# Attention and gated MLP on one core: the fifth pair of heads split for the product with V

## The chip, the cores and the metric

The kernel runs on one core of one Trainium2 chip. The metric is device time in microseconds; the median of 3 runs before the change is 799.14 us (799.07 to 799.27). The engines are named as the profile names them: PE (TensorE, with PEld for its weight loads), DVE (VectorE), ACT (ScalarE), POOL (GpSimd) and SP (SyncE, which issues most transfers).

## The reference

```python
def _attn_ref(q, k, v, f):                       # q, k, v: 8 x 8 x 576 x 64
    scores = (1 / sqrt(D)) * q @ k.T
    cum = cumsum(log(clip(f, 1e-4, 1)))
    scores = where(causal, -1e9, scores + cum[..., :, None] - cum[..., None, :])
    attn = exp(scores - max(scores))
    attn = attn / (sum(attn) + 1e-9)
    return attn @ v

def _moe_ref(x, w_in, w_spatial, b_spatial, w_out):   # x: 8 x 576 x 512, d_ff 1024
    h = relu(x @ w_in)
    u, v = h[..., :512], h[..., 512:]
    v_n = (v - mean(v)) / sqrt(var(v) + 1e-6)
    v_s = einsum('ts,bsd->btd', w_spatial, v_n) + b_spatial[None, :, None]
    return (u * v_s) @ w_out
# result: _moe_ref of attn_out, its heads laid side by side
```

## The kernel before

The 64 heads are worked in 32 pairs `P`, four to a batch, and each batch's gated MLP (`moe`) follows on its four pairs. A pair goes through `scores` for each of its two heads (four tiles of 128 to 512 key columns, on PE into PSUM tiles `sc`, then DVE takes maximum and mask at L345 and ACT the exponential at L347, into `tt`), `scores_tail` for the last 64 queries of both heads (`tl`), `transposes` (PE turns `tt` into PSUM tiles `tp`), `evac` (the tiles `tp` go to SBUF), and `attend`, the product with V, into `x0` and `x1`. POOL divides the probabilities by their sums at L355, L375 and L378. In batch 0 there are three buffers for `sc` and for `tp`, later two.

The product with V is done in one of two ways. Pairs below `NF` keep probabilities (`ef`) and V (`vraw`) in float32; each tile `tp` is copied by either DVE or ACT, in turn (L386), and each matmul stands in the trace as two records. From `NF` on, both are split into a rounded and a remaining part: ACT casts `tp` to `eh` (L390), DVE subtracts it to get `el` (L391), ACT casts V (L321) and POOL subtracts (L322), which gives `vt` with hi and lo of each head side by side. Then `eh` and `el` are each multiplied with `vt`, and the two halves of the result, on different partitions of PSUM, are added by one more DVE instruction for each of `x0` and `x1` (L452), beyond the L450 that all pairs have.

While attention runs, PE's MoE matmuls (`ps`) lie between its steps. The weights `w_in` and `w_out` come as float64 and are converted piece by piece (`conv64`: L162 on ACT, L163 to L169 on DVE, L171 on POOL, L172 on ACT, L173 on POOL), so that DVE has this work besides its own until about 160 us. The last four pieces are those of `w_out`, which the tiles of the output product (`ps<-wo`) need.

The program is written with generators: `step` calls attention and `moe` in turn, by their progress. But the order of instructions on each engine is set by a scheduler, which goes by its own times of the instructions. Each engine then works its list in order. `after` ties the start of some instructions to marks such as the exponential of a given pair.

Of the kernel before, what the change touches and what calls it, by code (L numbers as in the profile page):

```python
# [16 lines left out]
DRAM = bass.MemoryType.DRAM  # L17

BIG = 1.0e9
NF = 5  # L20
NQ = 4
LEAD = 0.25
S = 576
# [15 lines left out]
def attn_gmlp_kernel(ctx: ExitStack, tc: tile.TileContext, qk, v, f, w_in, w_sp, b_sp, w_out, out):  # L39
# [268 lines left out]
    def read_vals(P):  # L308
        tag = "vt" if P < NF and P % 2 else "vraw"
        vts[P] = wk.tile([128, 5, 2, D], F32, name="vraw", tag=tag)  # L310
        after(SY.dma_start(out=vts[P], in_=v[P]), ("dma", P, 1))

    def prep_v(P):
        for p in range(P, min(P + 2, NF)) if P < NF else (P,):
            if p not in vts:
                read_vals(p)
        if P < NF:
            return
        vraw = vts[P]
        vt = wk.tile([128, 5, 4, D], F32R, name="vt", tag="vt")  # L320
        A.copy(vt[:, :, 0:4:3, :], vraw)  # L321
        G.tensor_tensor(out=vt[:, :, 1:3, :], in0=vraw, in1=f32(vt[:, :, 0:4:3, :]), op=ALU.subtract)  # L322
        vts[P] = vt
# [34 lines left out]
    def scores_tail(P):  # L358
# [14 lines left out]
        V.reciprocal(sm[:, 0:1], sm[:, 0:1])  # L373
        if P >= NF:
            G.tensor_scalar(out=tl[:, S:640], in0=tl[:, TL:S], scalar1=sm[:, 0:1], scalar2=1.0,  # L375
# [8 lines left out]
    def evac(P, ps, sel):  # L384
        if P < NF:
            (V.tensor_copy if nev[0] % 2 == 1 else A.copy)(sel(ET["f"]), ps)  # L386
            nev[0] += 1
            return
        h_ap, l_ap = sel(ET["h"]), sel(ET["l"])
        A.copy(h_ap, ps)  # L390
        V.tensor_tensor(out=l_ap, in0=ps, in1=f32(h_ap), op=ALU.subtract)  # L391

    def transposes(P, h):
        if P == NF and h == 0:
            ET["h"] = cst.tile([128, 2, 1600], F32R, name="eh", tag="eh")
            ET["l"] = cst.tile([128, 2, 1600], F32R, name="el", tag="el")
        for c in range(NB):
            n = 512 - 128 * c
            tp = PS['t'].tile([128, 512], F32, name="tp")
            for i in range(c, NB):  # L400
                T.transpose(out=tp[:, (i - c) * 128:(i - c + 1) * 128],  # L401
                            in_=tt[h][:, TOFF[i] + 128 * c:TOFF[i] + 128 * c + 128], identity=ident)
            e0 = EOFF[c]
            evac(P, tp[:, 0:n], lambda e: e[:, h, e0:e0 + n])
            yield 107 * (NB - c)
# [309 lines left out]
```

## Time and profile before

| | |
|---|---|
| median of 3 runs | 799.14 us (799.07 to 799.27) |
| profiled execution, its own time | 797.53 us |
| its span | 795.7 us, granted clock 0.993 |
| busy | PE 778.9, DVE 556.6, ACT 534.9, POOL 476.4 us |
| PE, records of the float32 product with V | 140, from 20.9 to 104.7 us |
| PE, records of the split product | 378 with `eh`, 324 with `el`, from 118.4 us on |

A line of the trace gives start, duration, engine, line, operation, result and operands, with `x` and the count where equal ones follow each other; a bracket names idle time ahead and what ended it. Durations of matmuls overlap, so work on PE is counted from one start to the next.

### The profile page before, as it was taken

To read this page: it belongs to the slowest core of one execution; us is meant where nothing else is said; L and a number is where in the kernel's file an instruction comes from. 1 tells how busy PE (TensorE), PEld (TensorE's weight loads), DVE (VectorE), ACT (ScalarE), POOL (GpSimd) and SP (SyncE) were. 2 spreads that over 40 slices of the span, in tenths; PEclk is the share of its full clock that TensorE was granted. 3 is DMA by queue.
4 is the path that set the end of the run, shared out by engine and by line. 5 is a ranking of instruction groups with operands and counts; after the bars stand their busy time and mean duration, and the time that the engine had idled before them with its cause. 6 is when DMAs were issued, how large, how long until landed. Compare 5 with 4: busy or idle time off the path is not lost.

```text
span 795.7 us, 15502 instructions
## 1 busy us (share of the span) xinstructions
PE 778.9 (98%) x4980; PEld 702.3 (88%) x4981; DVE 556.6 (70%) x1665; ACT 534.9 (67%) x1418; POOL 476.4 (60%) x660
## 2 busy tenths in 40 slices
PE   8999989899999999999999999999999999999997
PEld 4767779798999989998999989999899988998996
DVE  7889778975767667766866668766787658674421
ACT  7787678675777777667766668766686767764431
POOL 5777798664865647465655647554776537643251
PEclk9999999999999999999999999999999999999999
DMA  9967744566454565365454555564555465320001
GB/s 246 239 185 185 188 119 121 119 168 171 103 123 119 153 152 142 102 148 136 104 143 129 133 145 114 131 170 135 141 134 138 108 164 134 78 75 14 28 1 67
DMA packets 41713, 103.48 MB, mean 130 GB/s; under 512 B 6831, under 2 KB 8879, under 8 KB 41568
## 3 DMA queue, kind: packets, MB, share of 16 engines
q1 hardware_dynamic: 41306, 101.96, 49.7%
q8 instruction: 40, 0.66, 0.4%
q10 hardware_dynamic: 326, 0.53, 0.3%
q14 instruction: 41, 0.34, 0.1%
HBM read 39.42 MB, written 10.68 MB: 63 GB/s over the span
## 4 chain that ended last, share of the span: by engine, by line
PE 86%; DVE 6%; ACT 3%; POOL 2%; issue 2%; DMA 1%; ACTq 0%; POOLq 0%; DVEq 0%
PE ps L260 45%; PE sc L260 16%; PE x L260 12%; PE tp L401 8%; PE tp L260 2%; PE tp L414 2%; DVE tt L345 1%; POOL tt L355 1%; DVE el L391 1%; DVE xl L450 1%; DVE wa L163 0%; ACT eh L390 0%; DVE vx L545 0%; ACT tt L347 0%; ACT hi L278 0%
## 5 line engine op out<-in xcount | busy, mean ns | idle before, releaser
L355 POOL TENSOR_SCALAR tt<-tt,sm 128x128 f32<-128x128 f32 (+3 forms) x256 | 142.0, 573 | 74.9 <-DVE sm L351 56.4
L345 DVE CUSTOM_DVE_ANT_0 tt<-sc,zm 128x128 f32<-128x128 f32 (+3 forms) x256 | 122.8, 486 | 85.0 <-PE tp L401 63.4
L390 ACT CAST eh<-tp 128x512 fp32r<-128x512 f32 (+1 forms) x270 | 111.4, 426 | 75.4 <-PE tp L401 50.2
L347 ACT ACTIVATE tt<-tt,nm 128x128 f32<-128x128 f32 (+3 forms) x256 | 144.4, 565 | 23.7 <-DVE nm L345 21.9
L391 DVE TENSOR_TENSOR el<-tp,eh 128x512 fp32r<-128x512 f32 (+1 forms) x270 | 127.2, 485 | 26.2 <-ACT eh L390 23.8
L401 PE MATMUL tp<-ident,tt 128*128 128x128 f32 x640 | 111.6, 277 | 4.1 <-DVE el L391 4.1
L260 PE MATMUL sc<-ta 128*128 128x128 f32 (+1 forms) x336 | 109.1, 330 | 2.5 <-DVE nm L345 2.0
L260 PE MATMUL sc<-tb 68*128 68x128 f32 (+1 forms) x336 | 106.2, 320 | 0.0
L260 PE MATMUL x<-eh,vt 128*128 128x320 f32 (+4 forms) x378 | 102.5, 287 | 0.0
L593 POOL TENSOR_TENSOR gl<-u,gh 128x256 fp32r<-128x256 f32 x64 | 47.7, 745 | 87.7 <-ACT gh L592 78.1
L260 PE MATMUL ps<-xh,win 128*128 128x256 f32 (+1 forms) x464 | 99.3, 304 | 0.4 <-ACT u L570 0.3
L280 POOL TENSOR_TENSOR lo<-raw,hi 128x640 fp32r<-128x640 f32 (+1 forms) x56 | 84.2, 1525 | 16.1 <-ACT hi L278 15.9
L260 PE MATMUL ps<-win,xh 128*128 128x512 f32 x296 | 90.6, 396 | 0.0
L260 PE MATMUL x<-el,vt 128*128 128x256 f32 x324 | 90.1, 303 | 0.0
L401 PEld LDWEIGHTS tp<-ident,tt 128*128 128x128 f32 x640 | 76.3, 141 | 14.2 <-issue 2.7
L449 ACT CAST xh<-x 64x256 fp32r<-64x256 f32 (+1 forms) x128 | 49.8, 394 | 42.3 <-PE x L260 40.3
L260 PEld LDWEIGHTS ps<-xh,win 128*128 128x128 f32 x464 | 76.3, 192 | 2.0 <-ACT u L570 0.9
L260 PE MATMUL ps<-sph,vnh 128*128 128x256 f32 (+1 forms) x240 | 73.2, 305 | 0.4 <-ACT o L618 0.4
L260 PEld LDWEIGHTS x<-eh,vt 128*128 128x128 f32 x378 | 71.3, 190 | 2.5 <-POOL vt L322 0.3
L260 PE MATMUL ps<-wo,gh 128*128 128x512 f32 x224 | 71.9, 405 | 0.0
L260 PEld LDWEIGHTS sc<-ta 128*128 128x128 f32 x336 | 64.3, 191 | 8.6 <-DVE nm L345 4.5
L260 PE MATMUL ps<-sph,vnl 128*128 128x256 f32 (+1 forms) x240 | 71.6, 298 | 0.0
(178 smaller groups left out, 1916.4 us busy)
## 6 DMA issues: line engine op xcount, KB each, us to landing
raw<-in_dram SPq DMA_DIRECT2D x28, 608.0 KB
ta<-hi SPq DMA_DIRECT2D x56, 304.0 KB
vraw<-in_dram SPq DMA_DIRECT2D x32, 320.0 KB
tb<-hi SPq DMA_DIRECT2D x56, 160.0 KB
ta<-lo SPq DMA_DIRECT2D x56, 160.0 KB
out_dram<-o SPq DMA_DIRECT2D x32, 256.0 KB
ta<-hi SPq DMA_DIRECT2D x56, 144.0 KB
tb<-lo SPq DMA_DIRECT2D x56, 144.0 KB
```

The lines of the kernel that those rows point to most:

```text
L260: last['mm'] = T.matmul(o, l, r, start=st, stop=sp)
L280: G.tensor_tensor(out=lo[:, c], in0=raw[:, c], in1=f32(hi[:, c]), op=ALU.subtract)
L345: V.tensor_tensor_reduce(out=t, in0=sc[:, 0:n], in1=zm[:, 640 - n:640], scale=-0.125, scalar=3.0e38, op0=ALU.add, op1=ALU.min, accum_out=n ...
L347: last["exp"] = last["exp", P, h, i] = A.activation(t, t, AF.Exp, bias=nm[:, i:i + 1], scale=-1.0, accum_out=se[:, i, 0:1])
L355: G.tensor_scalar(out=t, in0=t, scalar1=sm[:, i:i + 1], scalar2=1.0, op0=ALU.mult, op1=ALU.mult)
L390: A.copy(h_ap, ps)
L391: V.tensor_tensor(out=l_ap, in0=ps, in1=f32(h_ap), op=ALU.subtract)
L401: T.transpose(out=tp[:, (i - c) * 128:(i - c + 1) * 128], in_=tt[h][:, TOFF[i] + 128 * c:TOFF[i] + 128 * c + 128], identity=ident)
L414: T.transpose(out=tp[:, j * 128:(j + 1) * 128], in_=tl[:, c * 128:(c + 1) * 128], identity=ident)
L449: last[P, h] = A.copy(hi, ps[m0:m0 + 64, 0:n])
L450: V.tensor_tensor(out=lo, in0=ps[m0:m0 + 64, 0:n], in1=f32(hi), op=ALU.subtract)
L593: G.tensor_tensor(out=gl[j][:, 0:256], in0=g[:, 0:256], in1=f32(gh[j][:, 0:256]), op=ALU.subtract)
```

## The change

```diff
-NF = 5
+NF = 4
```

`NF` is the number of pairs whose product with V is done in float32. With 4, pair 4 (the fifth, the first of batch 1) is split as all later pairs are. For its two heads 14 float32 matmuls (28 records) become 26 split ones. Its ten evacuations on DVE or ACT (five each) become ten on ACT and ten on DVE, with one small DVE cast (L423). Added besides are a POOL instruction on `tl` (L375), the V cast on ACT and the subtraction on POOL, and four L452 on DVE. The tiles `eh` and `el` are first used one pair earlier. The tile `vt` takes the buffer in which pair 3 has its V. No transfer is added or removed.

The scheduler's order changes from the end of pair 3 (the first transposes of pair 4) on; PE's last 2139 rows are the same in both.

On POOL, at the first head of pair 4, before; `wa` and `win` belong to the conversion of `w_in`, `raw`, `hi` and `lo` to the split of queries and keys of a later pair:

```order
L173 TENSOR_TENSOR win_842<-wa,win_842 128x512
L171 TENSOR_TENSOR wa<-w_942,wa 128x512
L173 TENSOR_TENSOR win_949<-wa,win_949 128x512
L280 TENSOR_TENSOR lo<-raw,hi 128x640
L280 TENSOR_TENSOR lo<-raw,hi 128x576
L543 TENSOR_TENSOR mv<-mv,lnc 128x1
```

The same place now:

```order
L173 TENSOR_TENSOR win_840<-wa,win_840 128x512
L171 TENSOR_TENSOR wa<-w_941,wa 128x512
L322 TENSOR_TENSOR vt<-vraw,vt 128x5x128
L280 TENSOR_TENSOR lo<-raw,hi 128x640
L280 TENSOR_TENSOR lo<-raw,hi 128x576
L173 TENSOR_TENSOR win_948<-wa,win_948 128x512
```

The subtraction that makes `vt` of pair 4 stands behind L171, and the second L173 moves behind the split of queries and keys.

On PE, at the same time, before, from the end of a block of MoE matmuls on:

```order
L260 MATMUL ps<-win_578,xl 128x512
L401 MATMUL tp<-ident,tt_67 128x128 x2
L260 MATMUL x_1129<-ef,vraw 128x256
L401 MATMUL tp<-ident,tt_67 128x128
L260 MATMUL x_1129<-ef,vraw 128x128
L260 MATMUL sc<-ta 128x384
L260 MATMUL sc<-tb 128x384
L260 MATMUL sc<-ta 128x512
L260 MATMUL sc<-tb 128x512
L414 MATMUL tp<-ident,tl 128x128 x3
```

The same place now:

```order
L260 MATMUL ps<-win_578,xl 128x512
L260 MATMUL sc<-ta 128x384
L260 MATMUL sc<-tb 128x384
L260 MATMUL sc<-ta 128x512
L260 MATMUL sc<-tb 128x512
L401 MATMUL tp<-ident,tt_67 128x128 x3
L260 MATMUL x_1142<-eh,vt 128x256
L260 MATMUL x_1142<-el,vt 128x256
L260 MATMUL x_1142<-eh,vt 128x128
L260 MATMUL x_1142<-el,vt 128x128
L260 MATMUL sc<-ta 128x288
```

The product with V moves behind the two widest scores products, and the tail's scores and transposes stand behind it.

On PE again, later, between the first two tiles of the output product (`wo_1564` and `wo_1595` are the third pieces of `w_out`, before and now), before:

```order
L401 MATMUL tp<-ident,tt_67 128x128 x3
L260 MATMUL sc<-tb 128x256
L260 MATMUL ps<-wo_1564,gh 128x512
L260 MATMUL ps<-wo_1564,gl 128x512
L260 MATMUL ps<-wo_1564,gh 128x512
L260 MATMUL ps<-wo_1564,gl 128x512
L260 MATMUL sc<-ta 128x384
L260 MATMUL sc<-tb 128x384
L401 MATMUL tp<-ident,tt_67 128x128 x2
L260 MATMUL sc<-ta 128x512
```

The same steps of a head now:

```order
L401 MATMUL tp<-ident,tt_67 128x128 x3
L260 MATMUL sc<-ta 128x384
L260 MATMUL sc<-tb 128x384
L260 MATMUL sc<-ta 128x512
L260 MATMUL sc<-tb 128x512
L401 MATMUL tp<-ident,tt_67 128x128 x2
L260 MATMUL sc<-ta 128x288
L260 MATMUL sc<-tb 128x288
L260 MATMUL sc<-ta 128x288
L260 MATMUL sc<-tb 128x288
```

The four output matmuls that stood between the steps of this head are gone from it; they come later. Counted from the widest scores product of pair 7's second head on, PE had 23 output matmuls within the next two heads and one tail; now it has 8 within the next three heads and one tail.

## The prediction

> **What bounds the kernel now.** I read the page first, busy time and then slices.
>
> ```profile
> span 795.7 us, 15502 instructions
> PE 778.9 (98%) x4980; PEld 702.3 (88%) x4981; DVE 556.6 (70%) x1665; ACT 534.9 (67%) x1418; POOL 476.4 (60%) x660
> ...
> PE   8999989899999999999999999999999999999997
> ...
> DVE  7889778975767667766866668766787658674421
> ```
>
> PE fills the span but for a few slices before 170 us, and there DVE stands at 7 to 9 tenths. The windows put numbers on those slices (columns: length, busy us of PE, weight loads, DVE, ACT, POOL, then the granted clock).
>
> ```profile
> core 0: us, PE busy (x) PEld busy (x) DVE busy (x) ACT busy (x) POOL busy (x), PEclk, DMA share, GB/s
> ...
> 80.00:90.00 10.00, 9.37 (x55) 7.36 (x54) 6.72 (x22) 5.89 (x16) 8.12 (x9) 1.00 0.54 153
> 100.00:110.00 10.00, 8.85 (x50) 6.95 (x48) 6.20 (x19) 7.50 (x19) 9.10 (x14) 1.00 0.54 128
> 110.00:120.00 10.00, 9.07 (x57) 8.67 (x57) 9.70 (x23) 7.68 (x19) 9.36 (x6) 0.83 0.46 121
> 140.00:150.00 10.00, 10.00 (x71) 9.24 (x70) 9.81 (x27) 5.27 (x15) 7.25 (x8) 1.00 0.72 170
> 150.00:160.00 10.00, 6.76 (x38) 5.03 (x36) 9.04 (x24) 7.66 (x20) 6.46 (x9) 0.81 0.29 72
> 160.00:170.00 10.00, 9.96 (x59) 9.06 (x60) 8.03 (x28) 7.43 (x23) 6.95 (x9) 0.85 0.69 176
> 300.00:400.00 100.00, 99.42 (x669) 92.50 (x668) 71.48 (x213) 68.86 (x184) 60.64 (x88) 1.00 0.50 124
> ```
>
> From 300 to 400 us PE idles 0.6 us in 100, so late in the kernel only PE's own work counts. Between 150 and 170 us PE idles 3.3 us, and the clocks of 0.81 and 0.85 take another 0.19 and 0.15 of ten, 3.4 us: 6.7 us lost. There DVE is busy 9.04 and PE 6.76, so DVE is the bound. The changed order rewrites everything from the end of pair 3 (82 us) on, and meets the old order again in PE's last 2139 rows, word for word. So three terms make the sum: PE's work, waits near pair 4, and that DVE-bound stretch.
>
> **PE's work.** These rows show products with V: float32 heads of pairs 3 and 4, then a split head.
>
> ```profile
> 79.63 2.46 PE L260 MATMUL x<-ef,vraw 128*128 128x320 f32 x10
> 82.02 0.98 PE L401 MATMUL tp<-ident,tt 128*128 128x128 f32 x7
> ...
> 98.33 0.60 PE L260 MATMUL x<-ef,vraw 128*128 128x256 f32 x2
> 98.76 0.27 PE L401 MATMUL tp<-ident,tt 128*128 128x128 f32 x1
> 98.87 0.39 PE L260 MATMUL x<-ef,vraw 128*128 128x128 f32 x2
> 99.02 0.48 PE L260 MATMUL ps<-win,xl 128*128 128x512 f32 x1
> ...
> 134.03 0.36 PE L260 MATMUL x<-eh,vt 128*128 128x256 f32 x1
> ...
> 135.71 0.36 PE L260 MATMUL ps<-sph,vnh 128*128 128x256 f32 x1
> ```
>
> Matmuls overlap, so I count from start to start. A float32 product is two records. Ten for x1 take 82.02 - 79.63 = 2.39 us, the two of 256 columns 0.43 and the two of 128 columns 0.15: 2.97 us a head. A split head, 13 matmuls, takes 135.71 - 134.03 = 1.68. Two heads save 2.6 us; switching between kinds adds a little, and I take **-2.7 us**, between -2.4 and -2.8. Nothing covers PE here, so this is a true gain unless a wait takes it.
>
> **Waits near pair 4.** The V of pair 4 now needs an ACT cast and a POOL subtraction before the first product, and the ten evacuations of its probabilities each go through ACT and then DVE instead of one of them. In the new order POOL does the subtraction behind a weight conversion.
>
> ```profile
> 84.71 0.38 PE L401 MATMUL tp<-ident,tt 128*128 128x128 f32 x2
> ...
> 85.61 0.42 PE L260 MATMUL sc<-ta 128*128 128x384 f32 x1
> ...
> 86.53 0.49 PE L414 MATMUL tp<-ident,tl 128*128 128x128 f32 x3
> ...
> 84.94 1.28 POOL L171 TENSOR_TENSOR wa<-w,wa 128x512 f32<-128x512 f32 x1
> ...
> L375 POOL TENSOR_SCALAR tl<-tl,sm x27: 314/320/563, 100.7 to 712.4; 128x64 f32<-128x64 f32 x27
> ...
> L322 POOL TENSOR_TENSOR vt<-vraw,vt x27: 1554/1574/2011, 115.6 to 723.2; 128x640 fp32r<-128x640 f32 x27
> ...
> 88.30 0.44 PE L414 MATMUL tp<-ident,tl 128*128 128x128 f32 x2 [0.51 <-ACT ef L386]
> ...
> 109.85 0.41 PE L401 MATMUL tp<-ident,tt 128*128 128x128 f32 x2 [0.94 <-DVE el L391]
> ```
>
> PE: the MoE block ends at 84.71; the wide scores (86.53 - 85.61 = 0.92) and three transposes (0.3) bring it to 85.9. POOL: L171 starts at 84.94, 0.32 later for the added L375, ends at 86.5, and L322 takes 1.57: V is ready at 88.1. PE waits 2.2 us, in order, with the tail's scores and transposes queued behind it. What goes is the old idle time there (10 - 9.37 = 0.63, most of it the 0.51 at 88.30). That leaves **+1.6 us**. Below, it is 0 if POOL runs ahead of my count; above, 2.4 if nothing of the old wait goes. The wait at 109.85, where pair 5 is now the first to be split, I leave: pair 5 still has to wait for DVE there, only with two additions (L450, L452) ahead of it. The rest of the added DVE work, ten L391 for five copies, four L452 and a small cast, about 4.5 us, is covered there: DVE is busy 6.72 of 10 and 6.20 of 10 in two windows. ACT gains five casts and the V cast, about 3 us, under the same cover (5.89 and 7.50). If that cover fails, the transposes come late and this term is at its top. No DMA is added; SP's reads of V keep their place for pair 4 and move ahead for pair 5, both long before use.
>
> [...]
>
> **The stretch at 147 to 170 us.** Here the first two tiles of the output product wait for the conversions of w_out, and all later MoE matmuls stand behind them. The rows are the widest scores product of a head on PE, its evacuation on DVE, and one conversion step, L169, slow and quick.
>
> ```profile
> 146.11 0.40 PE L260 MATMUL sc<-tb 68*128 68x512 f32 x1
> 168.10 0.39 PE L260 MATMUL sc<-tb 68*128 68x512 f32 x1
> ...
> 149.97 0.68 DVE L345 CUSTOM_DVE_ANT_0 tt<-sc,zm 128x512 f32<-128x512 f32 x1
> 169.87 0.69 DVE L345 CUSTOM_DVE_ANT_0 tt<-sc,zm 128x512 f32<-128x512 f32 x1
> ...
> 156.56 1.70 DVE L169 SCALAR_TENSOR_TENSOR wa<-w,wa 128x512 f32<-128x512 uint32 x1
> ...
> 97.17 0.66 DVE L169 SCALAR_TENSOR_TENSOR wa<-w,wa 128x512 f32<-128x512 uint32 x1
> ...
> L391 DVE TENSOR_TENSOR el<-tp,eh 128x512 fp32r<-128x512 f32 (+1 forms) x270 | 127.2, 485 | 26.2 <-ACT eh L390 23.8
> L345 DVE CUSTOM_DVE_ANT_0 tt<-sc,zm 128x128 f32<-128x128 f32 (+3 forms) x256 | 122.8, 486 | 85.0 <-PE tp L401 63.4 <-PE x L260 9.3 <-PE sc L260 3.4
> L450 DVE TENSOR_TENSOR xl<-x,xh 64x256 fp32r<-64x256 f32 (+1 forms) x128 | 57.5, 452 | 18.4 <-ACT xh L449 15.4 <-PE ps L260 0.5
> L452 DVE TENSOR_TENSOR xl<-x,xl 64x256 fp32r<-64x256 f32 x108 | 48.9, 455 | 3.4
> ```
>
> Before, DVE needs 169.87 - 149.97 = 19.9 us there for two heads, one tail and one conversion; PE does them with 23 output matmuls between. In the new order three heads and a tail stand in the same place with only 8 such matmuls, and one more L169. A head's DVE work is four L345 at 0.486, four L391 at 0.485 and two each of L450 and L452 at about 0.45: 5.7 us, with small ones about 6.0. So DVE needs 19.9 + 6.0 + 0.7 = 26.6 us (0.7 being the quick L169; 1.7 if slow), and 24.8 if it has no idle time of its own. I take 26.0. PE's work in it, at the start-to-start distances of the rows above, is 3 heads of about 4.0 us (scores 1.3, of which the two widest 0.92; ten transposes at 0.1; product 1.7), a tail of 1.6, 8 matmuls of 512 columns at 0.23 and some switching: an estimate of 15.9. PE loses 26.0 - 15.9 = 10.1 instead of 6.7: **+3.4 us**, from +2.2 (24.8) to +4.9 (27.5).
>
> A stalled PE also runs slower afterwards, as the 0.83 and 0.85 in the windows show. [...]
>
> **Sum.** -2.7 + 1.6 + 3.4 = +2.3 us. The profiled execution took 797.5 us with its 795.7 span, 1.6 below the median of the runs, 799.14. So it would become 799.8, and the median 801.4.
>
> **Rivals.** First, the other side: the split is simply cheaper. It needs the DVE stretch to take no more than 22.6 us (PE's 15.9 plus the old 6.7). For it: the undisturbed distances of those DVE rows add up to 21.4, and the fourth conversion comes one head later than before, which thins DVE's work. Against: windows before show DVE at 9.81 and 9.04 with the same kind of work. With V waiting 0.7 us, the stretch neutral: -2.0, 797.1; with no wait at all 796.4; were the old 6.7 halved as well, 793. Second, the waits eat just the gain: V's wait of 1.6 and about 1.1 in the stretch, where DVE then takes 23.7 us, between its undisturbed rows and my count: 0.0, 799.1. Third, the clock: a new stall of 2.2 us at 86 and a longer one at 150 end in slow matmuls, as 110 to 120 us does at 0.83 (1.7 us of ten): +2.3 + 1.7 = +4.0, 803.1; with both other terms at their tops (-2.7 + 2.4 + 4.9 + 1.7), 805.4.
>
> **How the numbers follow.** A run of this kernel can't be told from no change within 0.2%, 1.6 us. My forecast, with the clock rival as its upper end (800.7 to 805.4): 0.50. Waits eat the gain (797.5 to 800.7): 0.28. Cheaper split (below 797.5): 0.22, most of it at 796.4 to 797.5. The likeliest case is 801.4; its own range is 800.7 to 805.4; the range over cases is 796.4 to 805.4.
>
> **What would show it.** Right: x<-ef is gone after 82 us and PE has 2.6 us less work; at about 86 us PE waits some 2 us for POOL vt L322; three heads near 147 to 174 us with DVE at 9 tenths or more and PE below 7. Wrong: no PE wait at 86; PE over 8 tenths between 150 and 170; DVE idle there for lack of scores. The prediction falls if DVE isn't the bound in that stretch, since then the gain on PE is all that is left.

## The result and the profile after

With the fifth pair split the kernel takes 808.61 us (median of 4 runs, 806.45 to 809.72) against 799.20 us (799.07 to 799.74) before, measured beside it: the ratio is 1.0113 [1.0090, 1.0136], 9.4 us slower. The forecast was 801.4 us, slower by 2.3 us; the measured time lies above its own range (800.7 to 805.4) and above the range over all its cases. The profiled execution took 809.7 us, with a span of 807.9. That is 12.2 us over the span before, because that one lay 1.6 us below its median and this one 1.1 us above.

Page of the changed kernel, busy times and two of the slices:

```profile
span 807.9 us, 15519 instructions
...
PE 783.7 (97%) x4979; PEld 705.1 (87%) x4979; DVE 563.3 (70%) x1675; ACT 537.0 (66%) x1424; POOL 476.6 (59%) x662
...
PE   8999889979999999999999999999999999999997
...
DVE  7879799986666667766676668666687558764421
```

PE's slices dip between 80 and 120 us and between 140 and 180 us, as before, and the last of them is deeper. The windows of the changed kernel give the numbers (columns as in the prediction):

```profile
core 0: us, PE busy (x) PEld busy (x) DVE busy (x) ACT busy (x) POOL busy (x), PEclk, DMA share, GB/s
80.00:90.00 10.00, 7.96 (x42) 6.35 (x41) 7.18 (x20) 7.05 (x18) 8.74 (x11) 0.98 0.64 178
90.00:100.00 10.00, 9.10 (x49) 7.98 (x48) 6.88 (x24) 6.78 (x17) 7.35 (x11) 0.85 0.75 188
100.00:110.00 10.00, 8.57 (x47) 7.10 (x46) 9.09 (x22) 5.15 (x14) 6.48 (x7) 1.00 0.59 153
110.00:120.00 10.00, 8.59 (x49) 7.40 (x48) 9.87 (x22) 8.03 (x20) 9.92 (x13) 0.84 0.22 46
...
150.00:160.00 10.00, 8.22 (x52) 7.37 (x51) 9.62 (x29) 6.43 (x19) 6.58 (x9) 0.89 0.85 193
160.00:170.00 10.00, 8.50 (x52) 7.27 (x52) 8.59 (x30) 8.94 (x24) 9.30 (x11) 0.94 0.43 107
170.00:180.00 10.00, 8.11 (x40) 6.51 (x38) 9.20 (x29) 7.32 (x21) 6.35 (x10) 0.83 0.70 181
180.00:190.00 10.00, 9.20 (x64) 8.77 (x64) 5.84 (x21) 6.40 (x18) 7.83 (x9) 1.00 0.51 140
```

In both kernels PE loses time in two ways: it idles, and it runs for stretches of 3.41 us at a granted clock of 0.50, called half clock below. Scores products of 288 columns start 0.24 us apart in such a stretch (at 91 us) and 0.14 us apart outside (at 116 us), so I count as its cost, an estimate from that clock, half of the time in which PE is busy. Of the three such stretches before, one has PE idle for more than half of it (columns as above):

```profile
156.19:159.60 3.41, 1.60 (x5) 0.91 (x6) 3.32 (x6) 1.93 (x5) 2.72 (x3) 0.50 0.23 57
```

That makes 0.8 us beyond the idle time, and 1.7 us for a full one.

From 80 to 120 us PE idles 5.8 us (2.04 + 0.90 + 1.43 + 1.41), where it idled 2.7, and half clock takes 3.3 us (0.2 + 1.5 + 1.6), where it took 1.7. From 150 to 190 us PE idles 6.0 us and half clock takes 3.4: 9.4 us lost, where 5.8 were lost before (3.3 and 2.5). Over the whole span, but for half clock in the last 4 us, which both have, the account is:

- idle 24.2 us (807.9 - 783.7) for 16.8, +7.4;
- half clock 8.5 us (five stretches) for 4.2 (three), +4.3. One of the two added stretches lies at 55 us, ahead of the changed order, and comes in some executions only: the trace of e3 below, the same program up to there, hasn't got it;
- PE's work, its busy time less that loss, 775.2 us for 774.7, +0.5, where -2.7 was forecast.

The timeline of the changed kernel shows the stops (idle time ahead of a row in the bracket, with what ended it):

```profile
89.51 0.56 PE L260 MATMUL x<-eh,vt 128*128 128x256 f32 x1 [2.04 <-POOL vt L322]
...
105.81 0.39 PE L260 MATMUL x<-eh,vt 128*128 128x320 f32 x1 [1.30 <-DVE xl L452]
...
115.00 0.33 PE L401 MATMUL tp<-ident,tt 128*128 128x128 f32 x1 [1.13 <-DVE el L391]
...
162.39 0.40 PE L260 MATMUL sc<-ta 128*128 128x288 f32 x1 [0.66 <-DVE nm L345]
...
165.02 0.40 PE L260 MATMUL sc<-ta 128*128 128x288 f32 x1 [0.84 <-DVE nm L345]
...
171.20 0.50 PE L260 MATMUL sc<-ta 128*128 128x512 f32 x1 [0.68 <-DVE nm L345]
...
180.91 0.50 PE L260 MATMUL ps<-wo,gh 128*128 128x512 f32 x1 [0.80 <-POOL wo L173]
```

The first is the forecast's wait for V. The second is new: in pair 4's second head, the first of the products into `x1` waits until DVE's L452 has read `x1` of the first head, a step that only split pairs have. Behind 150 us there are eight stops of 0.5 to 1.2 us, one instruction each, where the kernel before had three, of 1.03, 0.40 and 1.81 us.

### The profile page after: what moved, and what is told of

It reads as the page before. It is cut to its first block, busy times and chain, and to the rows that moved or that the text cites. A ratio compares the mean times of both kernels' runs of the same rounds, so it can differ in the third digit from the quotient of the medians.

```text
span 807.9 us, 15519 instructions
## 1 busy us (share of the span) xinstructions
PE 783.7 (97%) x4979; PEld 705.1 (87%) x4979; DVE 563.3 (70%) x1675; ACT 537.0 (66%) x1424; POOL 476.6 (59%) x662
## 4 chain that ended last, share of the span: by engine, by line
PE 78%; DVE 9%; POOL 3%; ACT 3%; DMA 2%; issue 2%; SPq 1%; POOLq 0%; ACTq 0%; DVEq 0%
PE ps L260 40%; PE sc L260 15%; PE x L260 12%; PE tp L401 7%; PE tp L260 2%; PE tp L414 2%; DVE vx L545 2%; DVE tt L345 1%; DVE el L391 1%; POOL tt L355 1%; POOL vt L322 1%; DMA tb<-lo 1%; DVE st L541 1%; DVE xl L450 1%; DMA tb<-hi 1%
## 5 line engine op out<-in xcount | busy, mean ns | idle before, releaser
L355 POOL TENSOR_SCALAR tt<-tt,sm 128x128 f32<-128x128 f32 (+3 forms) x256 | 138.8, 561 | 80.1 <-DVE sm L351 58.6
L345 DVE CUSTOM_DVE_ANT_0 tt<-sc,zm 128x128 f32<-128x128 f32 (+3 forms) x256 | 122.6, 485 | 81.0 <-PE tp L401 57.2
L390 ACT CAST eh<-tp 128x512 fp32r<-128x512 f32 (+1 forms) x280 | 115.5, 426 | 90.5 <-PE tp L401 60.2
L347 ACT ACTIVATE tt<-tt,nm 128x128 f32<-128x128 f32 (+3 forms) x256 | 144.3, 565 | 24.1 <-DVE nm L345 22.6
L391 DVE TENSOR_TENSOR el<-tp,eh 128x512 fp32r<-128x512 f32 (+1 forms) x280 | 131.8, 484 | 24.7 <-ACT eh L390 22.6
L401 PE MATMUL tp<-ident,tt 128*128 128x128 f32 x640 | 114.3, 281 | 4.1 <-DVE el L391 3.9
L260 PE MATMUL x<-eh,vt 128*128 128x256 f32 x392 | 107.8, 289 | 3.5 <-POOL vt L322 2.0
L260 PE MATMUL x<-el,vt 128*128 128x256 f32 x336 | 96.0, 307 | 0.0
L260 PEld LDWEIGHTS x<-eh,vt 128*128 128x128 f32 x392 | 74.8, 192 | 6.5 <-POOL vt L322 3.0
```

The source lines that it names most:

```text
L260: last['mm'] = T.matmul(o, l, r, start=st, stop=sp)
L345: V.tensor_tensor_reduce(out=t, in0=sc[:, 0:n], in1=zm[:, 640 - n:640], scale=-0.125, scalar=3.0e38, op0=ALU.add, op1=ALU.min, accum_out=n ...
L347: last["exp"] = last["exp", P, h, i] = A.activation(t, t, AF.Exp, bias=nm[:, i:i + 1], scale=-1.0, accum_out=se[:, i, 0:1])
L355: G.tensor_scalar(out=t, in0=t, scalar1=sm[:, i:i + 1], scalar2=1.0, op0=ALU.mult, op1=ALU.mult)
L401: T.transpose(out=tp[:, (i - c) * 128:(i - c + 1) * 128], in_=tt[h][:, TOFF[i] + 128 * c:TOFF[i] + 128 * c + 128], identity=ident)
```

## The experiments

Most of them hold an order. Each instruction is tied to the one that shall stand ahead of it on its engine, from a table written out from one of the two programs; this adds no wait between engines (names shortened):

```diff
+    for p, q in zip(seq, seq[1:]):      # seq: the wanted order on one engine
+        tc.add_manual_dep(tbl[q], tbl[p].name, DependencyInfo(NoSync, DATA), reason="order")
```

So the product and the order can be changed apart. "Old order" is that of the kernel before, "new order" that of the changed one. All were timed in five rounds beside the kernel before; the last columns are the difference to that kernel's median there, and the ratio.

| run | what | us | difference | ratio |
|---|---|---|---|---|
| changed | split, new order | 808.61 | +9.4 | 1.0113 [1.0090, 1.0136] |
| e1 | split, old order | 804.65 | +5.5 | 1.0075 [1.0057, 1.0093] |
| e2 | float32, new order | 812.56 | +13.4 | 1.0172 [1.0157, 1.0188] |
| e3 | changed, V earlier | 807.87 | +8.7 | 1.0117 [1.0101, 1.0132] |
| e4 | before, four late pairs float32 | 811.48 | +12.3 | 1.0165 [1.0147, 1.0184] |
| e5 | as e2, pair 5's V in its own buffer | 806.06 | +7.9 | 1.0098 [1.0080, 1.0116] |
| e6 | as e3, no el for pair 4 | 807.14 | +9.0 | 1.0120 [1.0099, 1.0141] |
| e7 | changed, quick w_out | 808.22 | +10.1 | 1.0131 [1.0109, 1.0153] |
| e8 | NF = 6 | 800.62 | +2.5 | 1.0037 [1.0023, 1.0050] |
| e9 | float32, old then new order | 813.44 | +14.5 | 1.0176 [1.0156, 1.0196] |
| e10 | as e1, V earlier | 804.37 | +5.5 | 1.0069 [1.0058, 1.0081] |
| e11 | changed, V wait filled | 808.88 | +10.0 | 1.0125 [1.0111, 1.0138] |
| e12 | before, waits filled | 796.04 | -2.9 | 0.9961 [0.9949, 0.9974] |
| e13 | split, new then old order | 808.06 | +9.5 | 1.0113 [1.0094, 1.0131] |
| e14 | split, old then new order | 819.37 | +20.8 | 1.0260 [1.0245, 1.0275] |
| e15 | as e6, all DVE relief | 805.66 | +7.1 | 1.0094 [1.0078, 1.0111] |
| e16 | as e10, waits filled | 801.74 | +3.2 | 1.0041 [1.0029, 1.0053] |
| e17 | float32, lead 0.24 | 800.94 | +2.0 | 1.0025 [1.0016, 1.0034] |
| e18 | split, lead 0.24 | 808.79 | +9.8 | 1.0122 [1.0103, 1.0141] |

### Order and product apart (e1, e2, e5)

e1: `NF = 4` and the table of the old order. 

> Pair 4 split (NF = 4), with every instruction that both kernels share held in the order of the kernel before on its engine; the split matmuls stand where the float32 ones stood, and the steps that only a split pair has (V's cast and subtraction, ten more evacuation steps, L452) are placed freely between them. Theory A, the new order makes the loss: the product's gain shows and only the wait for V stays, so 796.5 to 800.5 us. Theory B, the split pair's own steps make it wherever they stand: 805 to 809 us. PE's work alone would be -2.7 us.

It took 804.65 us, just below theory B's range and well outside theory A's. Rows of the timeline before, and of e1 behind them, at the same three places of the order:

```profile
84.71 0.38 PE L401 MATMUL tp<-ident,tt 128*128 128x128 f32 x2
...
111.88 0.44 PE L260 MATMUL sc<-ta 128*128 128x288 f32 x1
...
790.35 0.40 PE L260 MATMUL ps<-wo,gt 128*128 128x512 f32 x1
```

```profile
84.60 0.42 PE L401 MATMUL tp<-ident,tt 128*128 128x128 f32 x2
87.62 0.38 PE L260 MATMUL x<-eh,vt 128*128 128x256 f32 x1 [2.61 <-POOL vt L322]
...
95.83 0.30 PE L260 MATMUL x<-eh,vt 128*128 128x64 f32 x1 [1.27 <-DVE eh L423]
...
114.43 0.66 PE L401 MATMUL tp<-ident,tt 128*128 128x128 f32 x2 [1.39 <-DVE el L391]
...
117.76 0.44 PE L260 MATMUL sc<-ta 128*128 128x288 f32 x1
...
795.90 0.40 PE L260 MATMUL ps<-wo,gt 128*128 128x512 f32 x1
```

e1 is level at 84.6 us, 5.9 us behind at 111.9 us of the old time, and 5.6 us behind at the end. With the order held, the whole cost of the split pair arises in the 30 us from its start on, and the stretch behind 150 us loses nothing more.

e2: `NF = 5` and the table of the new order. 

> The counterpart: pair 4 in float32 (NF = 5), with every shared instruction held in the order of the changed kernel; the float32 matmuls stand where the split ones stood, and V of pair 5 is read and split freely. Theory A, the order makes the loss: 808.6 us less the wait for V of pair 4 (2.0 us idle and 1.7 us of half clock behind it) plus 2.7 us for the dearer product, 804 to 811 us. Theory B, the split pair's own steps make it: 798 to 801 us, as before.

812.56 us, a little above theory A's range. One stop in its timeline was made by the experiment: V of pair 5 can't be read before the float32 product of pair 4 has let go of the buffer.

```profile
116.12 0.58 PE L260 MATMUL x<-eh,vt 128*128 128x256 f32 x1 [4.40 <-POOL vt L322]
```

e5 takes that away:

```diff
-        vts[P] = wk.tile([128, 5, 2, D], F32, name="vraw", tag=tag)
+        vts[P] = (WU[0] if P == 5 else wk).tile([128, 5, 2, D], F32, name="vraw", tag=tag, bufs=1)
```

> Pair 4 in float32, in the order of the changed kernel as in the counterpart before, but V of pair 5 is read into a buffer of its own, so that its split needn't wait for the product of pair 4 (there PE waited 4.4 us for it). This leaves the order alone. Theory A (the new order costs by itself, about 5.3 us by that trace without the wait and its half clock): 803 to 807 us. Rival (all of that kernel's loss was the wait for V of pair 5): 798.5 to 801 us.

806.06 us: the new order costs 7.9 us with not one instruction of pair 4 changed. Split alone costs 5.5, the order alone 7.9, both together 9.4. They don't add up: the new order was made for the split pair's durations, and the float32 pair finds stops of its own in it (1.87 us for L391 at 115 us).

The same account for the four traces, in us:

| | pair 4 | order | idle | half clock | PE's work |
|---|---|---|---|---|---|
| before | float32 | old | 16.8 | 4.2 | 774.7 |
| e1 | split | old | 22.9 | 6.6 | 771.8 |
| e5 | float32 | new | 19.8 | 6.6 | 777.8 |
| changed | split | new | 24.2 | 8.5 | 775.2 |

In either order the split saves PE's work, 2.9 and 2.6 us, near the 2.7 of the forecast; what hides the saving in the changed kernel is the order, which adds 3.1 to 3.4 us of work. It shows on the same 880 products into the tiles `sc`: counted from start to start, without idle time and at full clock, they take 154.1 us before and 153.9 in e1, but 156.1 in e5 and 156.4 in the changed kernel. Single traces with the changed kernel's PE instructions in its order (changed, e3, e6, e7, e15) spread from 773.7 to 777.7 us of work, all above the two of the split in the old order (e1 771.8, e10 772.1), so the direction is clear, and the size is good to some 2 us.

### The price of the product (e4)

```diff
+NQ = 4; LATE = (10, 14, 18, 22)
...
-        if P < NF:
+        if P < NF or P in LATE:          # evac; prep_v, transposes_tail and attend likewise
```

> The kernel before, with pairs 10, 14, 18 and 22 also worked in float32, where PE hardly waits: it prices the product. By the forecast's count (1.3 us a head) eight heads add 10.4 us: 809.6 us (808 to 811). Rival, a split head saves much less than its matmuls' start-to-start distances say, as the changed kernel's PE busy time hints (783.7 against 778.9 us): 0.5 us a head or less, 799 to 803 us.

811.48 us: 12.3 us for eight heads, 1.5 us a head. Its page:

```profile
span 808.8 us, 15427 instructions
...
PE 790.2 (98%) x4988; PEld 707.3 (87%) x4989; DVE 540.0 (67%) x1625; ACT 527.0 (65%) x1394; POOL 469.3 (58%) x656
```

Of that, 1.8 us is idle time (18.6 us for 16.8), which leaves 1.3 us a head, as forecast (1.4 by the spans of the two traces).

### One wait less (e3, e10, e6)

e3, on POOL in the new order:

```diff
+L322 TENSOR_TENSOR vt<-vraw,vt
 L173 TENSOR_TENSOR win<-wa,win
 L171 TENSOR_TENSOR wa<-w,wa
-L322 TENSOR_TENSOR vt<-vraw,vt
```

> The changed kernel with its own order on every engine, but on POOL the subtraction for V of pair 4 (L322) stands two instructions earlier, ahead of L173 and L171 of the weights. If the wait for V (2.04 us at 89.5 us) and the half clock behind it (1.7 us) cost what they show: 804.9 us, or 806.6 us if only the wait goes. Rival: the time is only moved to the next wait, 808 to 809.5 us. By the forecast's term for this wait (1.6 us): 807.0 us.

e10 makes the same move in the old order. 

> The split pair 4 in the order of the kernel before (804.7 us), with the subtraction for V (L322) moved ahead of L173 and L171 on POOL. If PE's wait for V there (2.61 us at 87.6 us) is the price of the split pair: 800 to 802 us. Rival, as with the earlier V in the new order: PE finds the next wait (L391, L423 on DVE) and the gain is 1 us or less, 803.5 to 805 us.

Both rivals held, near enough: by the differences 0.7 us is gained in the new order, which the intervals don't tell from nothing, and nothing in the old. The wait for V goes, and the next one grows. Timeline of e10:

```profile
85.23 0.39 PE L260 MATMUL x<-eh,vt 128*128 128x256 f32 x1 [0.21 <-POOL vt L322]
...
90.29 0.41 PE L414 MATMUL tp<-ident,tl 128*128 128x128 f32 x2 [2.28 <-DVE el L391]
```

e6 then leaves out the DVE work that this second wait is for:

```diff
-        V.tensor_tensor(out=l_ap, in0=ps, in1=f32(h_ap), op=ALU.subtract)
+        if P > NF: V.tensor_tensor(out=l_ap, in0=ps, in1=f32(h_ap), op=ALU.subtract)
-            if P >= NF and cs[0] == 4:
+            if P > NF and cs[0] == 4:
-[ET["h"], ET["l"]][:2 if c < NB else 1]
+[ET["h"], ET["l" if P > NF else "h"]][:2 if c < NB else 1]
```

> As the kernel with the earlier V (807.9 us), in the same order, but pair 4's ten subtractions L391 and the cast L423 on DVE are left out; its products read eh twice instead of eh and el, so PE's work is the same (the result lacks the low part of pair 4's probabilities). Theory C, the added evacuation work on DVE is what PE waits for near pair 4: at least 4 us less, 801 to 804 us. Rival, V and L452 or the order of the rest hold PE there: 806 to 808 us.

+9.0 us, as the rival had it. By 118 us its trace is ahead of e3's, 115.24 for 117.91 us at the same matmul although it was 0.8 us behind at 70 us. Then PE waits for ACT (L570) and DVE (L539) of the MoE. Of the 3.5 us won, 2.3 are left at 125 us and 1.4 at 185 us of e3's time; by the medians nothing is left.

### The stretch behind 150 us (e7, e15)

e7:

```diff
-        V.tensor_scalar(out=a, in0=w, scalar1=0xFF800000, scalar2=None, op0=ALU.bitwise_and)
-        V.scalar_tensor_tensor(out=af, in0=lo, ...
+        if not temp: ...                 # both; temp is set for w_out alone
-        G.tensor_tensor(out=af, in0=wf, in1=af, op=ALU.add)
+        G.tensor_tensor(out=af, in0=wf, in1=wf if temp else af, op=ALU.add)
```

> The changed kernel in its own order, with two of the five DVE steps (L168, L169) of each of the four w_out pieces left out (the low words of w_out are dropped, POOL adds something else in their place), 1.1 to 1.2 us of DVE each. If DVE bounds the stretch at 150 to 185 us, as the forecast's term (c) has it, PE's loss there falls by about 4.5 us: 803.5 to 805 us. Rival, the stops there come from where scores and transposes stand on PE: 807 to 809 us.

No gain. In its timeline the same stops stand at the same steps, as long as in the changed kernel (0.66, 0.84 and 0.68 us there), and the last one has grown:

```profile
163.36 0.40 PE L260 MATMUL sc<-ta 128*128 128x288 f32 x1 [0.71 <-DVE nm L345]
...
165.98 0.40 PE L260 MATMUL sc<-ta 128*128 128x288 f32 x1 [0.84 <-DVE nm L345]
...
172.69 0.50 PE L260 MATMUL sc<-ta 128*128 128x512 f32 x1 [0.68 <-DVE nm L345]
...
181.47 0.50 PE L260 MATMUL ps<-wo,gh 128*128 128x512 f32 x1 [1.82 <-POOL wo L173]
```

These stops keep their length when DVE has some 4.5 us less to do, so they aren't DVE's throughput. Ahead of the L345 that ends the second of them DVE itself is idle, as long in the changed kernel as in e7 (rows in this order):

```profile
164.26 0.69 DVE L345 CUSTOM_DVE_ANT_0 tt<-sc,zm 128x512 f32<-128x512 f32 x1 [0.94 <-POOL tt L355]
```

```profile
165.22 0.69 DVE L345 CUSTOM_DVE_ANT_0 tt<-sc,zm 128x512 f32<-128x512 f32 x1 [0.94 <-PE x L260]
```

The profile names POOL in one and PE in the other as what ends that idle time, so what holds L345 there isn't settled.

e15 takes all of it at once: e3's move, e6's edit, and e7's edit for `win6` and `win7` too. 

> The changed kernel's order with all relief for DVE at once: V of pair 4 subtracted earlier on POOL, pair 4's ten L391 and its L423 left out (eh read twice), and the two DVE steps for the low words left out in the last six conversions (win6, win7, w_out): some 12 us of DVE less between 85 and 175 us (0.48 us each for L391, 1.1 us for a piece's two steps); the result lacks those low parts. If DVE's throughput sets the pace there and each single relief was only given back at the next DVE wait: 802 us or less. If the places of scores and transposes in PE's order set it, with waits for one instruction at a time: 805 to 808 us.

805.66 us: some 12 us less on DVE brought 2.3 us, as the rival had it.

### Half clock (e11, e12, e16)

Cut into cells of 3.41 us, the kernel before shows one of its half-clock stretches so:

```profile
core 0: us, PE busy (x) PEld busy (x) DVE busy (x) ACT busy (x) POOL busy (x), PEclk, DMA share, GB/s
108.40:111.82 3.42, 1.55 (x7) 0.74 (x7) 3.42 (x9) 3.42 (x9) 1.93 (x2) 1.00 0.00 0
111.82:115.23 3.41, 3.41 (x15) 3.41 (x14) 3.41 (x7) 2.43 (x8) 3.41 (x3) 0.50 0.06 6
115.23:118.64 3.41, 3.41 (x29) 3.41 (x29) 3.17 (x9) 2.54 (x6) 3.41 (x3) 1.00 0.93 271
```

A cell in which PE idles 1.87 us, a whole cell at 0.50, then full clock. The expectations below call this theory D: idle time of PE within one cell puts the next one at half clock. e12 fills waits of the kernel before with matmuls of zeros into a PSUM buffer that is free there:

```diff
+FILL = {(5, 0, 2): 4, (5, 0, 3): 2, (7, 0, 2): 1, (7, 0, 3): 8}
+    fillers = lambda *at: [T.matmul(x, zm[:, 0:128], zm[:, 0:512], start=True, stop=True) for x in [ps_a.tile([128, 512], F32, name="x0")] for _ in range(FILL[at])] if at in FILL else 0
-            tp = PS['t'].tile([128, 512], F32, name="tp")
+            fillers(P, h, c); tp = PS['t'].tile([128, 512], F32, name="tp")
```

> The kernel before in its own order, with fifteen matmuls of zeros in three of its waits: four and two ahead of the transposes of pair 5 at 109.85 and 110.77 us, one and eight ahead of those of pair 7 at 155.72 and 159.00 us. By theory D the cells at half clock at 111.8 and at 159.6 us go, and the one at 156.2 us stays (the wait of 1.03 us ahead of it isn't filled): 795.7 us. If they do no good: 799 us; if they are in the way of the waits' end, up to 800.5 us.

796.04 us, 2.9 us faster than before and the best version of this study. But for the last 4 us, no cell behind 80 us is at half clock any more, also not the one at 156.2 us that was expected to stay. Windows of e12 at the same place:

```profile
108.90:112.30 3.40, 3.16 (x19) 1.97 (x18) 2.61 (x7) 3.33 (x10) 2.59 (x5) 1.00 0.20 77
112.30:115.70 3.40, 2.92 (x17) 2.23 (x18) 3.40 (x10) 3.40 (x8) 2.65 (x2) 1.00 0.00 0
```

e11 puts nine such matmuls into the changed kernel's wait for V (`FILL = {(4, 0, None): 9}`, at the head of `attend`). 

> The changed kernel in its own order, with nine matmuls of zeros (512 columns bf16, 1.9 us by the start-up rows of the same kind) ahead of the first product of pair 4, where PE waits 2.04 us for V. They do no work; they keep PE busy. Theory D, PE's idle time within one 3.41 us cell makes the next cell run at half clock: the cell behind this wait stays at full clock, 1.7 us less, 806.9 us. Rival, the half clock has another cause: 808.6 to 809.5 us.

The cells at 89.6 and 116.9 us do stay at full clock (the only half-clock cells behind 80 us lie at 160 and 174), and at 120.4 us of the changed kernel's time e11 has gained 3.1 us on it beyond what it was ahead at 70 us. Then a wait of 1.34 us for DVE's L539 at 120.67 us and two half-clock cells in a row at 161 us take it back: 808.88 us. The theory of the cell held, its price didn't.

e16 fills the split pair in the old order (e10 with `(5, 0, 2): 6, (5, 0, 3): 2, (7, 0, 2): 1, (7, 0, 3): 9`). 

> Pair 4 split in the order of the kernel before, V subtracted earlier (804.4 us without fillers), and eighteen matmuls of zeros in the waits ahead of transposes of pair 5 (six, two) and of pair 7 (one, nine). If the half clock eats the split pair's gain, four of the five cells at half clock behind 80 us go: 804.4 - 6.8 = 797.6 us (796.5 to 799). If the time is given back at a later wait: 801 to 804.5 us.

801.74 us, 2.3 us gained by the differences, where 6.8 were hoped for. Behind 80 us one half-clock cell was left of five. So half clock is a part of the split pair's cost in the old order, not all of it.

### Where the order's cost lies (e9, e13, e14)

Each joins the two orders at a place near 112 us where both have issued the same instructions on PE. 

> Pair 4 in float32, every engine in the order of the kernel before up to the first scores of pair 6's tail (about 112 us) and in the order of the changed kernel from there on; at that cut both orders have issued the same instructions on PE. It places the cost of the new order (806.1 us where it holds throughout). If it arises behind the cut, in the stretch of 150 to 180 us: 803.5 to 807 us. If it arises ahead of it, near pair 4: 798 to 800.5 us.

> Pair 4 split, every engine in the order of the changed kernel up to the first scores of pair 6's tail (about 113 us), from there on in the order of the kernel before. At the cut both orders have issued the same instructions on PE. If the cost of the new order lies behind the cut, only the split pair's own waits remain, as in the old order throughout: 803.5 to 805.5 us. If it lies ahead of the cut: 807.5 to 809 us.

> The opposite mix, pair 4 split: the order of the kernel before up to about 113 us, that of the changed kernel behind it. If the new order costs behind the cut (4 to 6 us beyond the 804.5 us of the old order throughout): 808 to 811 us. If not: 804 to 805 us.

813.44, 808.06 and 819.37 us. They don't answer the question: each made a long stop of its own at the join. In e13 it is this row, in e9 and e14 waits of 5.09 and 5.33 us for V of pair 5:

```profile
115.34 0.66 PE L401 MATMUL tp<-ident,tt 128*128 128x128 f32 x2 [3.76 <-DVE el L391]
```

### Other orders (e8, e17, e18)

e8 is `NF = 6`. 

> NF = 6: pair 5 also in float32, its order left to the scheduler. By the product's price alone (2.6 us dearer, as the kernel with four late float32 pairs showed): 801.8 us. If the DVE work it saves near 105 to 120 us removes the waits and the half clock there (4.4 us): 797.4 us. If any new order costs as the changed kernel's does (5 us): 804 to 808 us.

800.62 us: by the difference 2.5 us, what the product's price alone would give (2.6). That is in part chance: its trace has no half clock from 80 us on but in the last 3 us, and 4.0 us of idle time from 80 to 200 us, where the kernel before has 6.0, while PE's work, counted as above, is 5.6 us more.

e17 and e18 are the two kernels with `LEAD = 0.24`. 

> The kernel before with LEAD = 0.24 instead of 0.25: the same instructions in another order of attention and MoE behind about 87 us. If orders of the same work differ by several us (the order of the changed kernel with float32 cost 7.9 us): 802 to 808 us. If the order matters only where it fits the durations badly because pair 4 was replaced: 798 to 801 us.

> The changed kernel with LEAD = 0.24: pair 4 split, another order. If the split pair costs near pair 4 in any order (5.5 us in the old one): slower than the float32 kernel with the same lead by 3 us or more, and 804 to 811 us. If the loss was this one order's accident: within 2 us of that kernel, or faster by the product's 2.7 us.

800.94 and 808.79 us. With the same nudge the split pair costs 7.8 us (808.79 - 800.94, timed beside each other), more than the 3 us that were asked for, and the float32 kernel moved by 2.0 us only. The long stops stay at the steps where the two kernels of this case have them, so this is a small departure and weak evidence that the loss isn't one order's accident. Three orders that the scheduler made with pair 4 in float32 (before, e17 and e8, which has pair 5 in float32 too) lie within 2.5 us of each other, and both split ones 9 to 10 us above the best.

## Why the prediction was right on the sign and wrong on the size

**PE's work, -2.7 us.** The price was right: 1.3 us a head by e4, and 2.9 and 2.6 us for the pair with the order held. The term failed all the same, as it put the new order at nothing for PE's own work: the order adds 3.1 to 3.4 us (e5 against before, changed against e1), and +0.5 is what came. The 0.1 us that the term has for switching between the kinds of product was an estimate that no run shows apart. Part of the added work can be the ends of matmuls ahead of a stop, which no next matmul overlaps, with 13 stops for 8 between 80 and 200 us; that is only argued.

**Waits near pair 4, +1.6 us.** This is the step that failed most. The wait for V came where and how it was forecast: 2.04 us for L322, ending at 89.5 us, against 2.2 us ending at 88.1. But the term held this one wait alone. In the changed kernel +3.1 us of idle time and +1.6 of half clock came there, 4.7 in all, with a stated top of 2.4 and the half clock left to a rival. In the old order e1 has 8.5 us more of them (6.1 idle, 2.4 half clock). What was costed at nothing is what came: L391 and L423 on DVE (the cover of "6.72 of 10" was an average that didn't hold at the instruction that PE waits for); L452 (1.30 us), which the prediction weighed as more work for DVE ahead of pair 5, but not as what holds `x1` between the two heads of pair 4; and the half clock behind these stops.

**The stretch, +3.4 us.** The size was near: 9.4 us lost, where 10.1 were forecast, against 5.8 before. The 6.7 of the prediction counts 0.9 us twice, as PE is busy only 1.60 us of the half-clock stretch at 156.2 us. The reason given for it, that DVE needs 26 us for its work there, is refuted by e7 and e15, so the nearness is in part luck. The prediction's own sign of being wrong is there too: PE over 8 tenths between 150 and 170 us (8.22 and 8.50). PE stops for one instruction at a time, probably because the new order has fewer output matmuls between the steps of a head; no run puts them back. And this term was taken as all that the order does, while e5 puts the order alone at +7.9 us: by its trace 3.0 of idle time, 2.4 of half clock and 3.1 of PE's work.

**L391.** With 384 columns it took 545 ns each between 80 and 200 us, 553 before (15 instructions for 12), so the added ones didn't come slower. The waits come from their number and from where they fell.

**The clock.** It was a rival, at 1.7 us, from the 0.83 of one window; one more cell with PE busy throughout costs as much. The changed kernel has one more behind 80 us in the profiled execution, four for three, and one more at 55 us. e11 and e12 show that these cells come from the stops: filled, they go.

**Rivals.** "The split is simply cheaper" fell. It needed the stretch at 22.6 us or less and a V that waits 0.7. "Waits eat just the gain" was right in kind, and by far too small.

**Open.** What makes PE's own work longer in the new order, and which chain sets the pace of the new order when DVE has 12 us less to do: e15 is still 7.1 us over, with stops for L345, L366, the MoE's L539 and POOL's L173.

## What to carry to other kernels

Where one engine is full and its order is fixed ahead, a cheaper step on it is worth its price only if nothing that feeds it gets longer: count the stops that the longer feeders make, each with its idle time and, here from about 1.2 us on, with what it does to the clock (in the changed kernel a stop of 1.20 us ending at 54.66 us had a cell at 0.50 behind it, one of 1.30 us ending at 105.81 us had none). Where a scheduler makes the order, a change of one duration changes the order too, and that has a price of its own (7.9 us here with the work unchanged): hold the order and change the work, and the reverse, to tell them apart. Don't sum such waits one by one, nor hope to win them back one by one: taking away V's wait, DVE's work or a half-clock cell of the changed kernel gained 0.7 us at most each, and V's move with all the DVE work 2.3, since the next wait stood right behind. What did pay was to keep PE busy through its waits with matmuls of zeros in the kernel before (796.0 us); in the changed kernel it brought nothing (808.9 us).

## What the runs showed of the hardware

The half clock comes in cells of 3.41 us on a fixed grid: in the changed kernel they begin at 55.44, 89.57, 116.88, 157.84 and 174.90 us, within 0.04 us of 10, 8, 12 and 5 times 3.41 us apart. I laid this grid over all 20 traces of the study and summed PE's idle time for each cell from 20 us on. Of 50 cells with 1.4 us or more, 46 were followed by a cell at half clock; of 39 with 1.1 to 1.4 us, 22; of 4,428 with less, 21, most of them right behind another half-clock cell. So a stop costs its own length, and up to 1.7 us more if it fills some 40% of a cell; the same stop cut in two by the grid may cost nothing more. In e1 the wait of 2.61 us for V is cut into 1.43 and 1.17 us, and no half clock follows; the 2.04 us of the changed kernel lie in one cell, and the next is at 0.50. The executions of one kernel differ in this way too: those of e7 took 805.4 us at a granted clock of 0.996 up to 810.9 us at 0.987, and those of the kernel before, which has three such cells in its trace, 797.2 us at 0.995 to 801.1 us at 0.991 over all its runs. Idle time of 1.2 to 2 us in a cell was often enough: in the changed kernel 1.20 us in the cell from 52.02 us and 2.04 us in the one from 86.16 us, in the kernel before 1.87 us in the one from 108.40 us, each with a cell at 0.50 behind it.
